# Small products of one pair of blocks and of the pair before in one stretch of TensorE's work instead of two

## The chip, the cores and the metric

The kernel runs on one core of a Trainium2 chip. The time is what the device needs for one launch, in microseconds; the lower the better. The median of three runs of the kernel before is 523.09 us (522.92 to 523.13).

## What is computed

A gated linear attention (4 batches, 8 heads, 768 steps, head size 48) whose output is the input of a feed-forward layer with a squared ReLU (3072 tokens, 384 wide, 2048 inside). q, k, v and alpha come as float32, the two weights as float64, which the kernel converts; the state of the attention is 48 x 48 for each batch and head.

```python
for t in range(S):
    state = alpha[:, :, t, :, None] * state + np.einsum('bhd,bhe->bhde', k[:, :, t], v[:, :, t])
    y[:, :, t] = np.einsum('bhd,bhde->bhe', q[:, :, t], state)
x = y.transpose(0, 2, 1, 3).reshape(B * S, H * D)
h = np.maximum(x @ w_in, 0.0)
return h * h @ w_out
```


## The kernel before

**Blocks and groups.** The 768 steps are cut into chunks of 128. A chunk of one batch is a block; there are 24, block n being chunk n // 4 of batch n % 4. Four blocks make a group of 512 tokens, and the six groups (g = 0 to 5 in the code, first to sixth in words) go one after the other through the feed-forward layer. The attention of the blocks of the next group is done in between, in pairs of blocks.

**The order is written out by hand.** Every instruction goes to its engine's queue in the order of the program text. The feed-forward layer of a group is a list of units with a cost (`layer_in`: 16 tiles of h, 1.05 + 0.53 each; then `layer_out` or `out_plain`: sums of the output, about 1.08 each). The attention of a pair is a list of events with a due time in the same units, made by `attention` from the table `PLAN` (`EARLY` for the first pairs). `weave` goes through the units and puts each event ahead of the first unit at whose start its time has come. A unit is near 1.3 us of TensorE in the first group, where products are plain float32, and in the later groups, which multiply three split parts. The numbers of the table `AT` are the starts of the pairs: in `'g': (2.2, 15.0)` those of two pairs in the third to fifth group.

**A pair in the attention.** `ln`, `sp`, `cs`, `eb`, `ei`, `mk`, `mq` turn alpha into running products and scale q and k by them; `turn` transposes q and k of both blocks (32 transposes of 64 x 64, L482), and ScalarE copies them out of PSUM. Then come the small products:

- `scores` (L365 to L375): 16 products a block, k against q, 48 x 64 by 48 x 64, into two PSUM banks called sckv;
- `state_sums` (L389 to L400): 16 products a block, k against v, into the other halves of the same two banks (8 in the last chunk of a batch, blocks 20 to 23);
- `masked`, `sums_copied`, `next_state`: VectorE takes the scores through a mask into `am`, adds the sums to the state (`us`), and makes the next state;
- y of a pair (`product` in `y_begin`, L349 to L357): 32 products with the states (`s`, `us`), 16 with the half of `am` that lies on the same rows (`inner` with h = e) and 16 with the other half (h = 1 - e), into two banks for the pair.

A product here is two weight loads and two matmuls in the records of TensorE. The second 16 of `inner` change the rows of TensorE that write a bank; an empty GpSimd instruction (L456) that waits for the last of the first 16, and that the first of the second 16 waits for, keeps them apart.

`ga(a, n)` issues scores, sums, mask and copy of block n, then y of pair a up to the first half of `inner`, then `next_state(n)`. `gb(a, n)` issues the second half of `inner` of pair a, and then all of the products of block n + 1. With n the first block of a pair and a = n - 2 the pair before, one pair makes two stretches of small products: `ga` at 10 units after the pair's start, `gb` at 12.5, with large products of the feed-forward layer between (2.35 times 9.5 and 10.5 units in the first group). After `gb` come the copies of y into x on ScalarE (`ev_part`, four parts of about three copies, L515). With `ga` and `gb` go loads on SP's queue: k of block n + 3, v of n + 2 and n + 3, k of n + 4, and they wait there until the tile that they overwrite has been read (three tiles of k, four of v).

PSUM has eight banks, all of one pool: a tile of h takes one, y of a pair two, a block's sckv two, the transposes four, and the output layer holds four through its whole length.

Of the kernel before, what the change touches and what calls it, by code (L numbers as in the profile page):

```python
# [15 lines left out]


GB = 4
AT = {'evs': 0.4, 'lead': 4, 'post': 3, 'w_first': (46.0, 49.5, 53.0), 'wstep': 1.6, 'w_in_at': 2, 'w_in_by': 3.4, 'room1': 22, 'room': 25, 's0': 4, 'ahead': 6, 'late': 2, 'xs': 0.2, 'g0': (-0.5, 19.5, 28.0), 'sc0': (2.35, 2.35, 2.35), 'g1': (2.5, 19.5, 35.0), 'g': (2.2, 15.0), 'g1x': 50, 'gx': 46, 'g0x': 55.5, 'k0': 2, 'h0': 18, 'k1': 4, 'h1': 4, 'h1by': 2, 'evs0': 0.8, 'tp': 'ADMD', 'tp1': 'ADAD', 'split': 8, 'o0': (40, 47), 'o1': (), 'o2': (23, 26, 29, 35, 42, 36), 'str1': 24, 'ga': 10, 'gb': 12.5}


RUN = {0: 128, 32: 32, 64: 64, 96: 32}
# [3 lines left out]
def kernel(  # L26
# [12 lines left out]
    nc = tc.nc  # L39
    B, H, S, D = q.shape  # L40
# [36 lines left out]
    NW = 8  # L77
# [384 lines left out]
    def gb(a, n):  # L462
# [7 lines left out]
        if n is not None:  # L470
            for f in (scores, state_sums, masked, sums_copied, next_state):
                f(n + 1)

    def turn(n):

        for m in (n, n + 1):
            ps = blk[m]["T"] = [bank(m, "T", (2, NP, 64)) for _ in range(2)]
            for i, x in enumerate("kq"):
                rows = tile_of(x, m).rearrange("a h d -> a (h d)")
                for p in range(NP):  # L480
                    for h in range(2):
                        nc.tensor.transpose(  # L482
                            out=ps[h][:, i, p, :], in_=rows[HALF[h], 128 * p : 128 * (p + 1)],
                            identity=ident[HALF[h], HALF[h]],
                        )
# [275 lines left out]
    def layer_out(g):  # L761
        posts = [(0, in_post, (n,)) for n in range(NJ + 2 - AT["post"], NJ)] if g else []
        plain = NW - AT["k0"] if g == 0 else NW - AT["k1"] if g == 1 else 0
        first = 2 * plain
        units = [(1, out_plain, (p, t, plain)) for p in range(plain) for t in range(GB)]
        if plain:
            for i, x in enumerate(posts):
                units.insert(1 + 2 * i, x)
            posts = []
        if plain == NW:  # L770
            for t in range(GB):
                units.append((0, lambda t: store(g, t, out_tile(t)), (t,)))
            return units
        ahead = AT["ahead"]
        split = [f for i in range(0 if plain else AHEAD, NJ - first) for f in splits_of_h(first, i)]
        if g == 0:
            split = [f for i in range(NJ - first) for f in [(0, split_h, (first + i, 0)), (0, diff_h, (first + i,))]]
        if plain:
            at = AT["h0" if g == 0 else "h1"]
            for i in range(min(AHEAD, len(split) // 2)):  # L780
                units[at:at] = split[0:2]
                del split[0:2]
                at += 2 + AT["h1by"]
        for _ in range(min(AT["s0"], len(split) // 2)):
            units += [split.pop(0), split.pop(0)]
        for n in range(first, NJ):
            units.append((1.08, out_x, (n, first)))
            if posts:
                units.append(posts.pop(0))
            while split and NJ - (len(split) + 1) // 2 <= n + ahead and (  # L790
                split[0][1] is diff_h or split[0][2][1] - AHEAD - MORE <= n - first
            ):
                units += [split.pop(0), split.pop(0)]
        ps = list(range(plain, NW))
        steps = [ps] if g == NG - 1 else [ps[i : i + 2] for i in range(0, len(ps), 2)]
        for pair in steps:
            units += [(0.27 * len(pair), out_y, (g, pair, t, pair[-1] == ps[-1])) for t in range(GB)]
        return units
# [87 lines left out]
        (3.0, "cs1 eb1 ei1"),  # L886
    ) + tuple(x for x in PLAN if x[0] > 3)

    def attention(pairs, scale):


        out = []
        for t, n0, after, *last in pairs:
            for at, fs in EARLY if n0 < SPLIT else PLAN:
                for f in fs.split():
                    w = t + (AT[f] if scale == 1 and f in ("ga", "gb") else at) * scale
                    if f in ("ga", "gb"):
                        given = n0 - 2 if after else None, None if last or n0 >= NBLK else n0
                        out.append((w, {"ga": ga, "gb": gb}[f], given))
                    if f == "gb" and after:  # L900
                        for p in range(NP):
                            out.append((w + AT["evs" if scale == 1 else "evs0"] * p, ev_part, (n0 - 2, p)))
                    if last:
                        continue
                    if f == "ga" and n0 + 3 < NBLK:
                        out.append((w, load, (n0 + 3, "k")))
                    elif f == "gb":
                        for m, x in ((n0 + 2, "v"), (n0 + 3, "v"), (n0 + 4, "k")):
                            if m < NBLK:
                                out.append((w, load, (m, x)))  # L910
                    elif f == "turn":
                        if n0 < NBLK:
                            out.append((w, turn, (n0,)))
                            for m in range(n0 + 2, min(n0 + 4, NBLK)):
                                out.append((w, load, (m, "q")))
                    elif f != "ga" and n0 < NBLK:
                        n = n0 + int(f[-1])
                        out.append((w, steps[f[:-1]], (n,)))
                        if f[:-1] == "cs" and n + 2 < NBLK:
                            out.append((w, load, (n + 2, "a")))  # L920
        return sorted(out, key=lambda x: x[0])

    def weave(units, events):
# [12 lines left out]
    def plain_out(g):  # L936
        n = NW - AT["late"]
        units = [(1, ffn_out, (g, t, i)) for i in range(n) for t in range(GB)]
        return units + [(1, ffn_out, (g, t, i)) for t in range(GB) for i in range(n, NW)]

    units = [(2, ffn_in, (0, j)) for j in range(2, NJ)]
    units += layer_out(0) if AT["k0"] else plain_out(0)
    events = [(3.4 * i, next_weights, (3 + i,)) for i in range(2 * NW - 3)]
    events += [(3.4 * i + 1.5, convert_second, (3 + i,)) for i in range(-1, 2 * NW - 3)]
    events += [(0, load, (GB + 1,)), (1.0, load, (GB + 2, "k"))]
    for p, at in enumerate(AT["w_first"]):
        events += prepare(at, "i", p)
    t0, t1, t2 = AT["g0"]
    for pair, scale in zip(((t0, GB, False), (t1, GB + 2, True), (t2, GB + 4, True) + (True,) * (len(AT["g1"]) == 3)), AT["sc0"]):
        events += attention([pair], scale)  # L950
    events += splits_of_x(AT["g0x"], 1)
    order = [*range(NW - AT["k0"], NW), *range(NW - AT["k1"], NW - AT["k0"])]
    order += range(NW - max(AT["k0"], AT["k1"]))
    for p, at in enumerate(AT["o0"]):
        events += prepare(at, "o", order[p])
    weave(units, sorted(events, key=lambda x: x[0]))
    hid.clear()
    acc.clear()

    def stream(g):  # L960
        if g == NG:
# [8 lines left out]
    def stream_out(n, xs="ld"):  # L970
        todo.extend((x, "o", p) for x in xs for p in range(NW - n, NW))
        pump()

    for g in range(1, NG):
        events = []
        if g + 1 < NG:
            n = GB * (g + 1) + 2
            *ts, t0, t1 = AT["g1" if g == 1 else "g"]
            pairs = [(t, n - 2, False) for t in ts] + [(t0, n, True), (t1, n + 2, True)]
            events += attention(pairs, 1)  # L980
            events += splits_of_x(AT["g1x" if g == 1 else "gx"], g + 1)
        if g == 1:
            m = len(AT["w_first"])
            for p in range(m, NW):
                events += prepare(AT["w_in_at"] + AT["w_in_by"] * (p - m), "i", p)
            for i, at in enumerate(AT["o1"] + AT["o2"]):
                events += prepare(at, "o", order[len(AT["o0"]) + i])
            n = min(AT["k0"], AT["k1"])
            todo.extend(("l", "o", p) for p in range(NW - n, NW))
            events.append((AT["str1"], stream_out, (AT["k1"], "d")))  # L990
        kinds[0] = AT["tp1" if g == 1 else "tp"]
        room[0] = AT["room1" if g == 1 else "room"]
        events.append((26, stream, (g + 1,)))
        events.sort(key=lambda x: x[0])
        weave(layer_in(g) + layer_out(g), events)
        if g == 1:
            w_out.clear()
            hid.clear()
            acc.clear()


# [28 lines left out]
```

## Time and profile before

The profiled execution and the runs:

| | us |
|---|---|
| median of three runs | 523.09 |
| span of the profiled execution, first to last instruction | 520.6 |
| TensorE busy in it | 510.8 |
| VectorE busy | 366.0 |
| ScalarE busy | 313.0 |
| mean granted TensorE clock | 1.000 of full speed |

The span leaves out what lies around the first and last instruction, so it stands 2.5 us below the median of the runs. The groups of instructions that the change moves, from the profile's fifth part:

| line | what | count | busy, us |
|---|---|---|---|
| L372 | matmuls of the scores | 768 | 16.5 |
| L395 | matmuls of the sums | 704 | 15.5 |
| L352 | matmuls of y, all forms | 1472 | 61.1 |
| L515 | copies of y on ScalarE | 132 | 47.2 |

Busy times of matmuls overlap and are not their share of the span; the starts are 6 to 15 ns apart within a stretch, against 174 ns for a 128 x 384 product of the output layer and 227 ns for a 128 x 512 product of the input layer. In the list of the chain that ended last, a line has the start in us, the duration in us, and engine, tile, line and count.

### The profile page before, as it was taken

The page shows a single profiled execution, that of the slowest core. Times are in us where ns is not written, and L with a number is a line of the kernel's source. Part 1 is how long each engine was busy: PE and PEld are TensorE (multiplying, and loading weights), DVE is VectorE, ACT ScalarE, POOL GpSimd, SP SyncE. Part 2 cuts the span into 40 slices and gives each one's busy share as a digit, 9 for nine tenths or more (in the row PEclk, how much of TensorE's full clock was granted, in tenths as well). Part 3 has the DMA queues.
Part 4 walks back from the last instruction along what each step waited for, and adds up shares of the span by engine and source line. Part 5 has one row for each costly group of instructions (what it writes and reads, how often), then busy time and mean ns, then how long its engine had stood idle before and what let it go on. Part 6 is the DMA issues. An engine that isn't in the chain of part 4 may idle for free.

```text
span 520.6 us, 12925 instructions
## 1 busy us (share of the span) xinstructions
PE 510.8 (98%) x5276; PEld 418.2 (80%) x5276; DVE 366.0 (70%) x631; ACT 313.0 (60%) x650; POOL 5.4 (1%) x29
## 2 busy tenths in 40 slices
PE   7989999999999999999999999999999999999997
PEld 4754455668887668988899988899988899988997
DVE  4798989979978787867597476587465476363861
ACT  4668785677888594575963275963275763164620
POOL 4000000000000000000000000000000000000000
PEclk9999999999999999999999999999999999999999
DMA  9999687244686787898884788964673534898201
GB/s 161 209 278 213 196 240 218 60 114 176 224 200 196 195 246 198 264 317 206 195 248 148 251 246 198 230 187 150 231 255 126 179 126 151 268 340 293 70 0 62
DMA packets 140995, 102.36 MB, mean 197 GB/s; under 512 B 111476, under 2 KB 114568, under 8 KB 140936
## 3 DMA queue, kind: packets, MB, share of 16 engines
q1 hardware_dynamic: 140936, 101.53, 68.3%
q8 instruction: 42, 0.69, 0.6%
q14 instruction: 17, 0.14, 0.1%
HBM read 84.18 MB, written 17.33 MB: 195 GB/s over the span
## 4 chain that ended last, share of the span: by engine, by line
PE 93%; DVE 2%; SPq 2%; DMA 1%; issue 1%; POOL 1%; ACT 0%; POOLq 0%; DVEq 0%
PE o L701 41%; PE h L622 32%; PE h L805 7%; PE y L352 4%; PE T L482 2%; PE sckv L372 2%; PE sckv L395 2%; PE cs L265 1%; DMA qk_lent<-in_q_dram 1%; SPq L303 1%; SPq L109 1%; PE cs L268 1%; PE cs L269 1%; DVE x L515 0%; DVE w_in L182 0%
## 5 line engine op out<-in xcount | busy, mean ns | idle before, releaser
L622 PE MATMUL h<-xa,wb 128*128 128x512 f32 x240 | 68.2, 392 | 0.0
L622 PE MATMUL h<-xl,wl 128*128 128x512 f32 x240 | 67.9, 391 | 0.0
L622 PE MATMUL h<-xd,wd 128*128 128x512 f32 x240 | 67.3, 396 | 0.0
L515 ACT COPY x<-y 32x256 f32<-32x256 f32 (+2 forms) x132 | 47.2, 366 | 25.4 <-PE y L352 20.1
L547 DVE TENSOR_TENSOR hid<-h,hid 128x512 f32<-128x512 f32 x40 | 27.6, 689 | 45.5 <-PE h L622 45.4
L701 PE MATMUL o<-wb,ha 128*128 128x384 f32 x160 | 54.6, 342 | 0.0
L701 PE MATMUL o<-w_out,hid 128*128 128x384 f32 x160 | 54.0, 491 | 0.0
L701 PE MATMUL o<-wd,hd 128*128 128x384 f32 x304 | 53.8, 334 | 0.0
L701 PE MATMUL o<-wl,hl 128*128 128x384 f32 x160 | 53.5, 335 | 0.0
L639 ACT ACTIVATE h<-h 128x512 f32<-128x512 f32 x40 | 23.3, 582 | 49.7 <-PE h L622 49.7
L622 PEld LDWEIGHTS h<-xl,wl 128*128 128x128 f32 x240 | 45.1, 188 | 10.0 <-DVE xl L547 0.4
L701 PEld LDWEIGHTS o<-wd,hd 128*128 128x128 f32 x304 | 52.7, 188 | 0.3 <-DVE osb L737 0.3
L622 PEld LDWEIGHTS h<-xa,wb 128*128 128x128 f32 x240 | 44.6, 188 | 9.3 <-ACT xa L596 0.2
L622 PEld LDWEIGHTS h<-xd,wd 128*128 128x128 f32 x240 | 44.2, 188 | 9.2
L701 PE MATMUL o<-wb,hx 128*128 128x384 f32 x144 | 48.7, 338 | 0.0
L701 PE MATMUL o<-wl,hx 128*128 128x384 f32 x144 | 48.1, 334 | 0.0
L701 PEld LDWEIGHTS o<-w_out,hid 128*128 128x128 f32 x160 | 29.8, 190 | 19.3
L637 ACT ACTIVATE hid<-h 128x512 f32<-128x512 f32 x40 | 24.0, 600 | 34.6 <-PE h L622 34.5
L805 PE MATMUL h<-x,w_in 128*128 128x512 f32 (+1 forms) x108 | 43.6, 552 | 1.2 <-ACT x L515 1.2
L596 ACT ACTIVATE ha<-hid 128x512 fp32r<-128x512 f32 x40 | 25.6, 639 | 25.5 <-DVE hx L547 16.1
L805 PEld LDWEIGHTS h<-x,w_in 128*128 128x128 f32 x108 | 19.9, 190 | 21.1 <-issue 17.2
L547 DVE TENSOR_TENSOR hl<-hid,ha 128x512 fp32r<-128x512 f32 x40 | 27.5, 688 | 10.1 <-ACT ha L596 10.1
(114 smaller groups left out, 879.7 us busy)
## 6 DMA issues: line engine op xcount, KB each, us to landing
wd<-do SPq DMA_DIRECT2D x36, 384.0 KB, 3.7
wl<-lo SPq DMA_DIRECT2D x34, 384.0 KB, 4.0
wl<-li SPq DMA_DIRECT2D x32, 384.0 KB, 3.5
wd<-di SPq DMA_DIRECT2D x32, 384.0 KB, 3.9
raw<-in_moe_w_in_dram SPq DMA_DIRECT2D x8, 768.0 KB, 5.6
raw<-in_moe_w_out_dram SPq DMA_DIRECT2D x8, 768.0 KB, 5.6
v_in<-in_v_dram SPq DMA_DIRECT2D x24, 192.0 KB, 4.7
out_dram<-osb SPq DMA_DIRECT2D x24, 192.0 KB, 1.9
```

What stands on the lines that cost most here:

```text
L352: ins = nc.tensor.matmul(out=ys[e][64 * half : 64 * half + D + G * e, m % 2, p // 2, t], lhsT=lhsT, rhs=rhs, start=(half, e) not in seen, ...
L372: nc.tensor.matmul(out=ps[e][HALF[h], 0, p, :], lhsT=ks[rows, p, HALF[h]], rhs=qs[rows, p, HALF[h]], start=True, stop=True, skip_group_che ...
L395: nc.tensor.matmul(out=ps[h][64 * e : 64 * (e + 1), 1, p, G:64], lhsT=tile_of("k", n)[HALF[h], 2 * p + e, :], rhs=tiles["v"][n % NV][HALF[ ...
L482: nc.tensor.transpose(out=ps[h][:, i, p, :], in_=rows[HALF[h], 128 * p : 128 * (p + 1)], identity=ident[HALF[h], HALF[h]],)
L515: copy(out=x[kk][to : to + m, t : t + 2], in_=blk[n]["y"][e][r : r + m, :, p // 2],)
L547: nc.vector.tensor_tensor(out=o, in0=x, in1=z, op=op)
L596: nc.scalar.activation(out=a, in_=x, func=AF.Copy, scale=NEAR)
L622: nc.tensor.matmul(out=acc["h", j], lhsT=here[w, "i", p][:, kk, jj * 128 : (jj + 1) * 128], rhs=x_parts[x][:, kk], start=start and kk == 0 ...
L637: nc.scalar.activation(out=hid[j], in_=x, func=AF.Copy, scale=E)
L639: nc.scalar.activation(out=x, in_=x, func=AF.Copy, scale=1.0 + E)
L701: nc.tensor.matmul(out=acc[t][:, 0:DM], lhsT=lhs[:, t * C : (t + 1) * C], rhs=rhs, start=start, stop=stop, skip_group_check=True,)
L805: nc.tensor.matmul(out=ps, lhsT=w[:, kk, c0 : c0 + 128], rhs=xT[g][kk][:, cols], start=(kk == 0), stop=(kk == KM - 1),)
```

## The change

A new function `joined(a, n)` issues in one go what `ga` and `gb` did in two: the banks of y are taken first, then scores and sums of block n, y of pair a up to the first half of `inner`, `next_state(n)`, scores and sums of block n + 1, the second half of `inner`, and `next_state(n + 1)`. Where there is no n it calls `ga` and `gb` one after the other.

`attention` now takes one pair, with a time `whole_at`: where it is given, `joined` stands at that time, and the loads and copies of y that went with `ga` and `gb` go with it; where it is not, `ga` and `gb` stay. The table says for which:

- first group: blocks 4 and 5 at unit 27 (`ga` was at 21.8, `gb` at 24.2); blocks 6 and 7 and the y of 6 and 7 stay as they are;
- second group: blocks 8 and 9 at 12.5 (12.5 and 15.0); blocks 10 and 11 with the y of 8 and 9 at 24.8, and the preparation of 10 and 11 starts at 15.0, not at 19.5 (29.5 and 32.0); blocks 12 and 13 stay as they are;
- third to fifth group: the first pair at 12.2 (12.2 and 14.7), the second at 24.8 (25.0 and 27.5); in the fifth group the second has no new block, only y.

All groups are now woven in one list, with the units' start of the group added to the times, and what was done between two groups (emptying tables, setting the kinds of tiles) are units that cost nothing.

```diff
-AT = {... 'g0': (-0.5, 19.5, 28.0), ... 'g1': (2.5, 19.5, 35.0), 'g': (2.2, 15.0), ...}
+AT = {... 'g0': ((-0.5, 4, False, True, 27), (19.5, 6, True, True), (28.0, 8, True, False)),
+      ... 'g1': ((2.5, 8, False, 12.5), (15.0, 10, True, 24.8), (35.0, 12, True)),
+      'g': ((2.2, 6, True, 12.2), (15.0, 8, True, 24.8)), ...}
...
+    def joined(a, n):
+
+        if n is None:
+            ga(a, None)
+            gb(a, None)
+            return
+        product = y_begin(a) if a is not None else None
+
+        def sums(m):
+            for f in (scores, state_sums, masked, sums_copied):
+                f(m)
+
+        sums(n)
+        if a is not None:
+            for h in range(1 if a < B else 0, 2):
+                for m, p, e in heads(a):
+                    rows = slice(64 * e, 64 * e + D)
+                    s = blk[m]["u" if h else "s"]
+                    product(m, p, e, s[rows, p, G * (1 - e) : 64], blk[m]["qs"][rows, p, HALF[h]], HALF[h])
+            for m, p, e in heads(a):
+                end = inner(product, m, p, e, e)
+            passed = nc.gpsimd.nop(nofuse=True)
+            dep(passed, end)
+        next_state(n)
+        sums(n + 1)
+        if a is not None:
+            for i, (m, p, e) in enumerate(heads(a)):
+                begin = inner(product, m, p, e, 1 - e)
+                if i == 0:
+                    dep(begin, passed)
+        next_state(n + 1)
...
-    def attention(pairs, scale):
+    def attention(t, n0, after, scale=1, begun=True, whole_at=None, turn_at=None):
...
+                if f in ("ga", "gb") and whole_at is not None:
+                    w = whole_at
...
+                if f == "ga":
+                    out.append((w, ga if whole_at is None else joined, given))
+                elif f == "gb":
+                    if whole_at is None:
+                        out.append((w, gb, given))
+                    if after:
                         for p in range(NP):
-                            out.append((w + AT["evs" if scale == 1 else "evs0"] * p, ev_part, (n0 - 2, p)))
+                            out.append((w + AT["evs" if scale == 1 else "evs0"] * p, ev_part, (old, p)))
...
+                if f == "ga":
+                    loads(w, (n0 + 3, "k"))
+                elif f == "gb":
+                    loads(w, (n0 + 2, "v"), (n0 + 3, "v"), (n0 + 4, "k"))
...
-        weave(layer_in(g) + layer_out(g), events)
...
+    weave(units, sorted(events, key=lambda x: x[0]))
```

More of the change, by code (lines that the diff above doesn't have):

```diff
@@ L18 @@
 GB = 4
-AT = {'evs': 0.4, 'lead': 4, 'post': 3, 'w_first': (46.0, 49.5, 53.0), 'wstep': 1.6, 'w_in_at': 2, 'w_in_by': 3.4, 'room1': 22, 'room': 25, 's0': 4, 'ahead': 6, 'late': 2, 'xs': 0.2, 'g0': (-0.5, 19.5, 28.0), 'sc0': (2.35, 2.35, 2.35), 'g1': (2.5, 19.5, 35.0), 'g': (2.2, 15.0), 'g1x': 50, 'gx': 46, 'g0x': 55.5, 'k0': 2, 'h0': 18, 'k1': 4, 'h1': 4, 'h1by': 2, 'evs0': 0.8, 'tp': 'ADMD', 'tp1': 'ADAD', 'split': 8, 'o0': (40, 47), 'o1': (), 'o2': (23, 26, 29, 35, 42, 36), 'str1': 24, 'ga': 10, 'gb': 12.5}
+AT = {'evs': 0.4, 'lead': 4, 'post': 3, 'w_first': (46.0, 49.5, 53.0), 'wstep': 1.6, 'w_in_at': 2, 'w_in_by': 3.4, 'room1': 22, 'room': 25, 's0': 4, 'ahead': 6, 'late': 2, 'xs': 0.2, 'g0': ((-0.5, 4, False, True, 27), (19.5, 6, True, True), (28.0, 8, True, False)), 'sc0': (2.35, 2.35, 2.35), 'g1': ((2.5, 8, False, 12.5), (15.0, 10, True, 24.8), (35.0, 12, True)), 'g': ((2.2, 6, True, 12.2), (15.0, 8, True, 24.8)), 'g1x': 50, 'gx': 46, 'g0x': 55.5, 'k0': 2, 'h0': 18, 'k1': 4, 'h1': 4, 'h1by': 2, 'evs0': 0.8, 'tp': 'ADMD', 'tp1': 'ADAD', 'split': 8, 'o0': (40, 47), 'o1': (), 'o2': (23, 26, 29, 35, 42, 36), 'str1': 24, 'ga': 10, 'gb': 12.5}
 RUN = {0: 128, 32: 32, 64: 64, 96: 32}
@@ L887 @@
     ) + tuple(x for x in PLAN if x[0] > 3)
-    def attention(pairs, scale):
+    def attention(t, n0, after, scale=1, begun=True, whole_at=None, turn_at=None):
         out = []
[L893 to L900, printed above, removed]
-                        for p in range(NP):
-                            out.append((w + AT["evs" if scale == 1 else "evs0"] * p, ev_part, (n0 - 2, p)))
[L903 to L920, printed above, removed]
@@ new lines, in attention, with loads @@
+        old = n0 - 2 if after else None
+        given = old, n0 if begun and n0 < NBLK else None
+        def loads(at, *which):
+            out.extend((at, load, (m, x)) for m, x in which if m < NBLK)
+        for at, fs in EARLY if n0 < SPLIT else PLAN:
+            for f in fs.split():
+                w = t + (AT[f] if scale == 1 and f in ("ga", "gb") else at) * scale
+                if f in ("ga", "gb") and whole_at is not None:
+                    w = whole_at
+                if f in ("turn", "kc0", "kc1", "qc0", "qc1", "br0", "br1") and turn_at is not None:
+                    w = turn_at + (at - 6.5) * scale
+                if f == "ga":
[4 more added lines that the diff above has]
+                    if after:
+                        for p in range(NP):
+                            out.append((w + AT["evs" if scale == 1 else "evs0"] * p, ev_part, (old, p)))
+                if not begun:
+                    continue
+                if f == "ga":
+                    loads(w, (n0 + 3, "k"))
+                elif f == "gb":
+                    loads(w, (n0 + 2, "v"), (n0 + 3, "v"), (n0 + 4, "k"))
+                elif n0 >= NBLK:
+                    continue
+                elif f == "turn":
+                    out.append((w, turn, (n0,)))
+                    loads(w, (n0 + 2, "q"), (n0 + 3, "q"))
+                else:
+                    n = n0 + int(f[-1])
+                    out.append((w, steps[f[:-1]], (n,)))
+                    if f[:-1] == "cs":
+                        loads(w, (n + 2, "a"))
@@ L939, in plain_out, with ended, begun @@
         return units + [(1, ffn_out, (g, t, i)) for t in range(GB) for i in range(n, NW)]
[L941 to L958, printed above, removed]
+    def ended(g):
+        hid.clear()
+        acc.clear()
+        if g == 1:
+            w_out.clear()
+    def begun(g):
+        kinds[0] = AT["tp1" if g == 1 else "tp"]
+        room[0] = AT["room1" if g == 1 else "room"]
     def stream(g):
@@ L972, in stream_out @@
         pump()
-    for g in range(1, NG):
-        events = []
-        if g + 1 < NG:
[L977 to L981, printed above, removed]
+    units = [(2, ffn_in, (0, j)) for j in range(2, NJ)]
+    units += layer_out(0) if AT["k0"] else plain_out(0)
+    units.append((0, ended, (0,)))
+    base = [0]
+    events = [(3.4 * i, next_weights, (3 + i,)) for i in range(2 * NW - 3)]
+    events += [(3.4 * i + 1.5, convert_second, (3 + i,)) for i in range(-1, 2 * NW - 3)]
+    events += [(0, load, (GB + 1,)), (1.0, load, (GB + 2, "k"))]
+    for p, at in enumerate(AT["w_first"]):
+        events += prepare(at, "i", p)
+    order = [*range(NW - AT["k0"], NW), *range(NW - AT["k1"], NW - AT["k0"])]
+    order += range(NW - max(AT["k0"], AT["k1"]))
+    for p, at in enumerate(AT["o0"]):
+        events += prepare(at, "o", order[p])
+    events += splits_of_x(AT["g0x"], 1)
+    for (t, n0, after, run, *other), scale in zip(AT["g0"], AT["sc0"]):
+        events += attention(t, n0, after, scale, run, *other)
+    for g in range(1, NG):
+        base.append(sum(u[0] for u in units))
+        at0 = base[g]
+        units.append((0, begun, (g,)))
+        units += layer_in(g) + layer_out(g)
+        units.append((0, ended, (g,)))
+        if g + 1 < NG:
+            for t, n0, after, *other in AT["g1"] if g == 1 else AT["g"]:
+                n0 = n0 if g == 1 else n0 + GB * g
+                other = [None if x is None else at0 + x for x in other]
+                events += attention(at0 + t, n0, after, 1, True, *other)
+            events += [(at0 + t, f, x) for t, f, x in splits_of_x(AT["g1x" if g == 1 else "gx"], g + 1)]
         if g == 1:
@@ L984 @@
             for p in range(m, NW):
-                events += prepare(AT["w_in_at"] + AT["w_in_by"] * (p - m), "i", p)
+                events += prepare(at0 + AT["w_in_at"] + AT["w_in_by"] * (p - m), "i", p)
             for i, at in enumerate(AT["o1"] + AT["o2"]):
-                events += prepare(at, "o", order[len(AT["o0"]) + i])
+                events += prepare(at0 + at, "o", order[len(AT["o0"]) + i])
             n = min(AT["k0"], AT["k1"])
[L989 to L994, printed above, removed]
-        weave(layer_in(g) + layer_out(g), events)
[L996 to L999, printed above, removed]
+            events.append((at0, lambda: todo.extend(("l", "o", p) for p in range(NW - n, NW)), ()))
+            events.append((at0 + AT["str1"], stream_out, (AT["k1"], "d")))
+        events.append((at0 + 26, stream, (g + 1,)))
+    weave(units, sorted(events, key=lambda x: x[0]))
 _INS = ['q', 'k', 'v', 'alpha', 'moe_w_in', 'moe_w_out']
```

## The prediction

> **What bounds the kernel now.** I read the page first, then the chain that ended last, then the timeline of TensorE in single stretches, and last the packets of the instruction queue.
>
> ```profile
> span 520.6 us, 12925 instructions
> ...
> PE 510.8 (98%) x5276; PEld 418.2 (80%) x5276; DVE 366.0 (70%) x631; ACT 313.0 (60%) x650; POOL 5.4 (1%) x29
> ...
> q8 instruction: 42, 0.69, 0.6%
> ...
> PE 93%; DVE 2%; SPq 2%; DMA 1%; issue 1%; POOL 1%; ACT 0%; POOLq 0%; DVEq 0%
> ```
>
> TensorE is busy throughout and is 93% of the chain: a microsecond taken from its order of work, or put into it, is one of the whole. The q8 line is how TensorE's program arrives: 42 packets of 0.69 MB, 16,384 bytes each; 10,702 recorded TensorE instructions over 42 is 255 a packet. I take blocks of 256.
>
> The chain at one stretch of the second group and two of the third, with a long run of plain work for comparison:
>
> ```profile
> 200.56 0.62 PE sckv L372 x32
> 201.19 0.45 PE sckv L395 x32
> 201.64 1.45 PE y L352 x86
> 203.09 0.96 issue
> 204.05 0.33 PE y L352 x3
> 204.38 3.00 PE o L701 x16
> ...
> 235.99 0.62 PE sckv L372 x32
> 236.62 0.45 PE sckv L395 x32
> 237.07 1.41 PE y L352 x92
> 238.49 2.95 PE h L622 x12
> 241.43 0.62 PE y L352 x31
> 242.06 0.46 PE sckv L372 x32
> 242.52 0.46 PE sckv L395 x30
> 242.98 4.32 PE h L622 x18
> ...
> 451.09 32.68 PE h L622 x144
> ```
>
> Two things are to be seen: what a break between small and large products costs, and a stop of 0.96 us that no semaphore ends.
>
> **What is saved.** The change drops one break per joined pair. The first 32 matmuls of a stretch take 0.62, the next 32 about 0.46: 0.16 for coming in. The 12 large ones between the two halves take 2.95 us against 12 x 32.68/144 = 2.72: 0.23 for getting going and draining. Together 0.39; by starts alone I read 0.36; I take 0.38. Nine stretches are joined: blocks 4 and 5 (first group), 8 and 9, and 10 and 11 (second), 14 and 16 (third), 18 and 20 (fourth), 22 and the y of 22 alone (fifth). In the last nothing stands between the two halves of y, and the wait for GpSimd's empty instruction (L456), hidden before by large products, is laid open: at 30.18 us, where the two halves already adjoin, that gap is 0.34. So eight breaks count: -3.0 us. In the others the 64 matmuls of the second block (0.92 us) hide the 0.34. Nothing is queued behind that instruction on GpSimd.
>
> **What is paid: instructions.** A product is two weight loads and two matmuls. A full joined stretch holds 128 products, 512 instructions, two whole blocks, in about 3.9 us (from block 20 on, where kv has one half, 448); before, the halves held 320 and 192, with 2.9 to 4.4 us of large products between.
>
> ```profile
> 204.05 0.19 PEld L352 LDWEIGHTS y<-am,v_in 64*48 64x48 f32 x3 [1.10 <-issue]
> ```
>
> The stop at 202.87 (1.18 us between starts) falls behind the 4,544th TensorE instruction, which is 18 x 256 - 64. With borders at 256k - 64, the fetches that fall into long runs of large products begin mostly 18 to 36 instructions ahead of their border, from 53 us to 513 us without drift: the count holds. The stretch at 200.49 is the only one of the old kernel that meets two borders (at its instructions 59 and 315) with small products alone between them. At the first border the fetch began 0.78 us after it was passed, took 0.96, and TensorE ran on 1.40 us after its end; small products reach the next border in 1.96. So the stop is 0.78 + 0.96 + 1.40 - 1.96 = 1.18. The stretch at 174.23 also has two (36 and 292), but its first was fetched before the stretch began, and nothing stops.
>
> Up to the start of each joined stretch the same TensorE instructions have run as before the old first half (some waits apart), so the borders are known, and for five of them the fetch itself is in the trace of before:
>
> - group 2, blocks 10 and 11: moved to stand before the output layer, five units of eight instructions earlier than at 174.23; border at 76, second at 332: with the 0.6 to 1.1 seen in most dense stretches, 1.2 us.
> - group 3, first: border at 213; 1.09 + 0.93 + 1.40 - 1.95 = 1.5. Second: border at 247; its own fetch began only 3.18 us after the border, with four weight transfers under way, which gives 3.8; from the smallest row (0.61, 0.88) 0.9. I take 2.2, nearer the other stretches, since the border is nine instructions from wrapping out of the stretch and a transfer there will start later.
> - group 4: borders at 142 and 176; 1.4 and 1.5.
> - group 5, first: border at 134; 0.61 + 0.88 + 1.40 - 1.95 = 0.9, I take 0.8 for its fewer kv products.
>
> The three short stretches (256 instructions) cross one border each: 0. Sum +8.6; ends 5.0 and 10.5. The stop at 200.49 belongs to a pair that stays in two stretches; I leave it.
>
> [...]
>
> **What is paid: banks and queues.** A stretch now holds six PSUM banks (two y, four sckv) beside three of h at unit 12.2: nine of eight. The last sckv takes a bank of the first block's, free when its sums are copied: in the trace 237.79 + 0.35 = 238.14 (VectorE L406), and TensorE would want it at 235.92 + 2.39 = 238.31. Cost 0; without that cover, 0.2 to 0.7 per stretch if VectorE is behind by one 0.69 us instruction.
>
> At unit 24.8 the copies of y (L515, 0.37 each, three to a part) come from 27.5 to 24.8 and two parts now stand on ScalarE ahead of the ReLU of h14 and of four splits of h, all waiting for the end of y. From the end of the stretch: 0.25 + 2.2 for copies, 0.6 ReLU (L656), 0.6 split, 0.69 VectorE rest: the fourth split is ready after 4.3 us; TensorE has three output units of 8 x 33.32/192 = 1.39 us (o L701 at 483.77 in the chain), with the start 4.3. So it arrives just in time, and with VectorE's 1.38 us per split plus one 0.69 post the eighth comes 0.4 late. Between 0 and 0.6 in groups 3, 4 and 5: +0.6, ends 0 and 1.8.
>
> SP: the two v loads and one k load move with the second half; v overwrites the v that the stretch reads (four tiles), so SP waits there, at unit 24.8 instead of 27.5, and one wd load behind it (issued at 260.84 before) comes some 2 us later; it is read in the last quarter of the layer, over 20 us on. Cost 0. In the first group the k load of block 7 goes from unit 21.8 to 27, three units (4 us) ahead of its multiply against a landing of 4.7 us; VectorE has over 5 us of weight conversion queued ahead of it there. Cost 0; uncovered, 1.
>
> Blocks 10 and 11 are prepared 4.5 units earlier, inside the loaded input layer of group 2. The old preparation of blocks 8 and 9 in that layer shows idle of 0.26 (transposes, 141.74) and about 0.3 (cumulative sums, 135): 0 to 0.6, I take 0.3. The single weave over all groups changes no order but of events that tie: 0.
>
> **Sum.** -3.0 + 8.6 + 0.6 + 0.3 = +6.5 us on a span of 520.6: 527.1. The median of the runs, 523.09, lies 2.5 above the span; so 529.6. Ends: 5.0 - 3.0 = +2.0, 525.1; 10.5 + 1.8 + 0.6 - 3.0 = +9.9, 533.0.
>
> **Rivals.** (1) Fetching hides behind the stretch, the stop at 203 us was something else or needs a rarer coincidence. For: only one stop in the trace; it is put down to nothing. Against: its place to the instruction and the fetch just before it. Then 523.1 - 3.0 + 0.6 + 0.3 = 521.0, down to 520.1. Faster. It decides if the second border costs under 0.3 us per stretch. (2) Fetches stop TensorE, but for less: half the borders have shifted by added or dropped waits, or the request goes out earlier in a longer stretch. Then +8.6 is 2 to 4, and the time 522.2 to 525.1. Against: at 134 to 213 the borders lie 40 and more instructions from where the stop vanishes (about 40 and 256). (3) The output layers of groups 3 to 5 starve behind the ScalarE queue, each 1.5 us and more, on top of the stops: 533.5. For: ScalarE is strictly in order, and stands idle 4.60 us at 265.88 only because its work was done early; against: the sum above meets the need within 0.4.
>
> **How the numbers follow.** Forecast 0.74, range 525.1 to 533.0; rival 1 0.14; rival 2 0.08; rival 3 0.04. The range that leaves out no more than 2 in 10 reaches from rival 2's lower end, 522.0, to 533.0. What differs by under 0.2% (1.05 us) can't be told from no change here. Faster: rival 1, 0.14. Same: the lower part of rival 2 and the upper edge of rival 1, 0.04. Slower: 0.82.
>
> **What would show it.** Right: six new pieces of "issue" of 0.8 to 3 us inside y or sckv of full stretches, none in the three short ones, each behind an instruction 256k - 64 and 1.4 us after a packet of q8 ends; one run of large products fewer per pair; h L622 and o L701 as before. Wrong: full stretches of 3.9 us without a gap, or gaps ended by a semaphore (VectorE: banks; GpSimd: L456; ScalarE: splits). The forecast is wrong most simply if TensorE holds more than two blocks.

## The result, and the profile after

The changed kernel takes 539.73 us (median of four runs, 537.10 to 541.26) against 523.00 for the kernel before on the same chip (522.41 to 523.13): a ratio of 1.0315, 95% interval 1.0285 to 1.0345. It is slower by 16.7 us. The profiled execution took 537.1, its span is 535.3: 14.7 more than before. The page, with the parts that were shown of before:

```profile
span 535.3 us, 12918 instructions
...
PE 513.1 (96%) x5276; PEld 418.6 (78%) x5276; DVE 366.1 (68%) x631; ACT 314.5 (59%) x650; POOL 5.4 (1%) x29
...
q8 instruction: 42, 0.69, 0.5%
...
PE 76%; DVE 8%; ACT 6%; issue 4%; DMA 2%; SPq 2%; DVEq 0%; POOLq 0%
```

No engine has more instructions than before, and TensorE is busy for 513.1 us against 510.8, yet its share of the chain fell from 93% to 76%. The rest is of two kinds: "issue" (4%, before 1%), and stretches in which the chain runs through VectorE and ScalarE (8% and 6%, before 2% and 0%). Through most of the latter TensorE still works, and only the wait at the end of each costs time. Both are to be seen in the chain through the third group:

```profile
239.42 1.35 PE y L352 x88
...
242.02 1.08 issue
243.11 0.58 PE y L352 x18
...
248.87 0.94 ACT a_in L244 x2
...
251.46 0.57 DVE lo L257
...
252.07 0.44 PE cs L269
252.52 5.48 PE h L654 x24
258.00 1.16 PE T L514 x32
259.15 4.34 PE h L654 x18
...
267.35 2.77 issue
270.12 0.33 PE y L352 x3
```

**The stops.** All six full joined stretches stop once, and each stop lies behind an instruction 256k - 64 of TensorE, the second border of the stretch. Between starts they last 1.35 us (at 171.20, second group), 1.30 (241.80) and 2.98 (267.13, third), 2.10 (325.98) and 2.44 (352.47, fourth) and 0.98 (411.03, fifth): 11.15 together. The old stop, now at 205.44, is 1.08. The three short joined stretches have none.

**The waits behind the stretches.** TensorE's own timeline after the first of these stops (start, duration, operation and, in brackets, idle time and what ended it):

```profile
250.57 0.34 PE L268 MATMUL cs<-hi,causal_r 128*128 128x384 f32 x1
250.74 0.34 PE L269 MATMUL cs<-lo,causal_r 128*128 128x384 f32 x1
251.48 0.44 PE L268 MATMUL cs<-hi,causal_r 128*128 128x384 f32 x1 [0.40 <-DVE hi L256]
252.07 0.44 PE L269 MATMUL cs<-lo,causal_r 128*128 128x384 f32 x1
```

Four cumulative sums of the next pair follow at steps of 0.17 us where nothing is late (as at 251.54 in the run with one joined pair below); here two steps are 0.74 and 0.59, a loss of 1.0. At 336.18 the same comes again (0.79 and 0.59, 1.04). What they wait for stands on ScalarE. First before, then after:

```profile
240.79 0.60 ACT L637 ACTIVATE hid<-h 128x512 f32<-128x512 f32 x1 [4.18 <-PE h L622]
241.29 0.93 ACT L244 ACTIVATE a_in<-a_in 128x384 f32<-128x384 f32 x2
242.24 1.13 ACT L515 COPY x<-y 32x256 f32<-32x256 f32 x3
```

```profile
243.71 3.33 ACT L547 COPY x<-y 32x256 f32<-32x256 f32 x9 [4.74 <-PE y L352]
247.06 0.60 ACT L669 ACTIVATE hid<-h 128x512 f32<-128x512 f32 x1
247.69 1.15 ACT L547 COPY x<-y 64x256 f32<-64x256 f32 x3
248.87 0.94 ACT L244 ACTIVATE a_in<-a_in 128x384 f32<-128x384 f32 x2
```

Before, the logarithm of alpha (`a_in`, L244) stood ahead of the copies of y, and ScalarE did it while TensorE ran the second stretch (from 241.43 in the chain of before). Now ScalarE has nothing to do for the whole joined stretch (idle 4.74 us), and then everything at once: twelve copies (4.5 us), and the logarithm behind them. From the end of y at 243.69 to the end of `lo` at 252.03 that is 8.3 us; TensorE has 30 large products in between, 6.9 us. The whole-trace list of waits says the same: ScalarE's copies waited 43.5 us for y, before 20.1.

In the output layers of the third to fifth group a product waits for a split of h, 0.43 us above the step of 0.17 each time (the other two at 365.08 and 441.45):

```profile
280.24 0.34 PE L733 MATMUL o<-wb,ha 128*128 128x384 f32 x1
280.85 0.44 PE L733 MATMUL o<-wl,hl 128*128 128x384 f32 x1 [0.27 <-DVE hl L579]
```

**By group.** From the starts of the first product of each layer: second group +2.3 us, third +5.5, fourth +5.7, fifth +1.2, sixth 0, first -0.5, and +0.5 ahead of the first layer: 14.7. The last is scatter: the change alters nothing there, and the first layer begins between 27.2 and 28.4 us over all the profiles here.

### The profile page after: what moved, and what is told of

The parts are those of the page before. It is cut to its first block, busy times and chain, and to the rows that moved or that the text cites. A ratio compares the mean times of both kernels' runs of the same rounds, so it can differ in the third digit from the quotient of the medians.

```text
span 535.3 us, 12918 instructions
## 1 busy us (share of the span) xinstructions
PE 513.1 (96%) x5276; PEld 418.6 (78%) x5276; DVE 366.1 (68%) x631; ACT 314.5 (59%) x650; POOL 5.4 (1%) x29
## 4 chain that ended last, share of the span: by engine, by line
PE 76%; DVE 8%; ACT 6%; issue 4%; DMA 2%; SPq 2%; DVEq 0%; POOLq 0%
PE o L733 33%; PE h L654 25%; PE h L837 7%; PE y L352 4%; ACT x L547 3%; PE T L514 2%; PE sckv L372 2%; PE sckv L395 1%; SPq L303 1%; DMA qk_lent<-in_q_dram 1%; DVE hx L579 1%; PE cs L265 1%; SPq L109 1%; DVE hd L632 1%; DVE hid L579 1%
## 5 line engine op out<-in xcount | busy, mean ns | idle before, releaser
L547 ACT COPY x<-y 32x256 f32<-32x256 f32 (+2 forms) x132 | 47.0, 366 | 48.8 <-PE y L352 43.5
L579 DVE TENSOR_TENSOR hl<-hid,ha 128x512 fp32r<-128x512 f32 x40 | 27.5, 687 | 7.4 <-ACT ha L628 7.4
```

The lines of the kernel that those rows point to most:

```text
L547: copy(out=x[kk][to : to + m, t : t + 2], in_=blk[n]["y"][e][r : r + m, :, p // 2],)
L579: nc.vector.tensor_tensor(out=o, in0=x, in1=z, op=op)
```

## The experiments

The theory: a stretch of small products that holds two instruction borders runs to the second before the next 256 instructions have come, and stops. It was tried by moving borders, in the changed kernel and in the kernel before; then the joins were cut down, and last the transfers beside a fetch were moved.

**Empty instructions ahead of the stretches.**

```diff
+        for _ in range(n):
+            nc.tensor.nop(nofuse=True)
...
+    for g, at, k in [(1, 0, 62), (1, 48, 138), (2, 14, 32), (2, 27, 150), (3, 14, 32), (3, 27, 213)]:
+        events.append((base[g] + at, pad, (k,)))
```

> The changed kernel with 627 empty TensorE instructions, at most two behind each large product, so that the 256-instruction borders fall near instruction 18 of each of the six full joined stretches (62, 138, 32, 150, 32 and 213 ahead of them). Fetch theory: the six stops of 1.0 to 3.0 us (11.1 in the trace) and the old one (1.1) all but vanish, the span goes from 535.3 to 523 to 525 and the time to 525 to 528. Rival, a wait for banks or for GpSimd: the stops stay where they are by product, at the same places of the stretch, and the time stays at 537 to 541 or grows by what the empty instructions cost.

Measured 538.19 (536.02 to 540.45), ratio 1.0296 [1.0258, 1.0335]. It tells nothing of borders: the profiled program has 12,918 instructions in 42 packets, as the changed kernel has. The empty instructions were not in it, and the stops lie behind the same instructions. It is a repeat of the changed kernel, and as such of use: the stop at 267.12 lasted 3.81 us here and 2.98 there, the two of the fourth group 1.51 and 1.38 here and 2.10 and 2.44 there, and the six together 10.4 and 11.15.

The same edit in the kernel before, 155 empty instructions:

```diff
+        events += [(at, pad, (k,)) for h, at, k in [(1, 48, 155)] if h == g]
```

> The kernel before with 155 empty TensorE instructions near the end of its second group, so that in its first stretch of the third group (320 instructions) the first border moves from 213 to 58 and a second one to 314. Fetch theory: a new stop of 1.0 to 1.8 us in y some 2.3 us after the start of that stretch, the one in the second group stays, time 524 to 525. Rival: no stop there, 522.5 to 523.5.

522.67 in a single run, 12,925 instructions as before, no new stop: inconclusive for the same reason.

**Copies of y later.** They come 2.5 units after a joined stretch, as far from its second half as in the kernel before.

```diff
-                            out.append((w + AT["evs" if scale == 1 else "evs0"] * p, ev_part, (old, p)))
+                            late = 0 if whole_at is None else 2.5
+                            out.append((w + late + AT["evs" if scale == 1 else "evs0"] * p, ev_part, (old, p)))
```

> The changed kernel with the copies of y 2.5 units later, where they stood before (14.7 and 27.5), stretches unchanged. Theory that ScalarE's order costs what the stops do not explain: the waits for the cumulative sums (1.3 at 251, 1.4 at 336) and the output layers' 0.6 at 280, 365 and 441 go, 3 to 5 us less than the changed kernel, 534 to 537; the stops stay. Rival, that the rest is only a consequence of the stops: no change, 538 to 541.

536.57 (536.27 to 536.99), ratio 1.0266 [1.0250, 1.0281]: 3.2 us under the changed kernel's first measurement, 1.6 under its repeat on this chip, whose interval overlaps this one. What the order on ScalarE costs in time is therefore not settled by this run, but its profile shows the waits. Those for splits in the output layers are gone, and with the logarithm ahead of the copies again so are the waits for the sums near 251 and 336 us. But in their place a product of h starts 0.98 us after the one ahead of it, at 251.01 (0.75 above its step), and again at 338.45. What ends its wait is a copy of y, the seventh of nine that now stand in a row on ScalarE:

```profile
252.00 0.95 PE L654 MATMUL h<-xa,wb 128*128 128x512 f32 x3 [0.65 <-ACT x L547]
```

The bunch on ScalarE is waited for at either place. The stop at 266.84 grew to 4.88 us in this execution, in the chain:

```profile
267.05 4.67 issue
271.72 0.33 PE y L352 x3
```

With the empty instructions as well, which again are not in the program, it is a repeat:

> Both edits. If the two causes add: 12 plus 3 to 5 less than the changed kernel, 521 to 525, at the time of the kernel before or under it. If the second is a consequence of the first: as with the borders moved alone, 525 to 528.

536.82 (533.61 to 538.18), ratio 1.0249 [1.0209, 1.0290]; the longest stop 3.94. The six stops sum to 11.4 and 12.0 in these two profiles.

**Borders moved by aligning addresses.** Instead of empty instructions, the program's addresses are aligned ahead of each full joined stretch, so that its first border lies at the stretch's instruction 18 or 19.

```diff
+    for g, at, k in [(1, 21.6, 200), (2, 9.0, 200), (2, 21.6, 200), (3, 9.0, 200), (3, 21.6, 200), (4, 9.0, 200)]:
+        events.append((base[g] + at, lambda k: nc.tensor.addr_align(256, offset=k, max_nops=0), (k,)))
```

> The changed kernel with six directives that align TensorE's program, each about 38 instructions ahead of a full joined stretch: slots up to the next place are filled and branched over, so that the first border lies at instruction 18 or 19 of the stretch, where large products still stand before it. (The empty instructions of the earlier runs never came into the loaded program.) Fetch theory: the six stops (11.1 us in the trace) fall to under 0.5 us each, the one at 205 goes too since its border moves to 3; span 523 to 526, time 524 to 529. Rival, banks or GpSimd: the stops stay at the same products, 536 to 541.

530.91 (528.16 to 533.42), ratio 1.0163 [1.0130, 1.0196]: 7.7 us above the kernel before, where it had been 16.7, without a change to any product, though not down to the 529 that was the upper end of the expectation. The program now takes 44 packets instead of 42. The second border now lies at instruction 275, and the stops there are 0.45, 0.16, 0.69, 1.45 and 1.13, with none in the sixth stretch; but the stretch ends only 20 instructions ahead of a third border, and TensorE stops there, in the middle of large products, 1.28, 1.15 and 1.28 us in three cases. The chain at the first stretch of the third group:

```profile
239.13 0.45 PE y L352 x31
239.58 1.81 PE h L654 x7
241.39 0.89 issue
242.28 0.85 PE h L654 x3
```

That a run of large products stops at the border too, once the fetch is late, is the strongest sign that the small products are not the cause as such, only the pace. Neither place of the borders that was tried keeps a stretch of 512 instructions free of stops.

> The same with the copies of y 2.5 units later as well. If ScalarE's order has a price of its own: 1 to 4 us less than with the directives alone, 520 to 525. If not: the same as those within 1.

Both edits together: 530.06 (528.32 to 530.34), ratio 1.0124 [1.0104, 1.0144]. The waits of 0.97 for a copy of y are back (249.49 and 331.37), the waits in the output layer gone. The 520 to 525 that was expected if ScalarE's order has a price of its own didn't come, and the 0.85 us to the run before are within the noise.

**The same in the kernel before, both ways.** One address is aligned there, so that the stretch of blocks 12 and 13 has its borders at 20 and 276 instead of 59 and 315:

```diff
+        events += [(at, lambda k: nc.tensor.addr_align(256, offset=k, max_nops=0), (k,)) for h, at, k in [(1, 42.6, 203)] if h == g]
```

> The kernel before with one directive, 33 instructions ahead of its only stretch that stops (200.49 in its trace), border from 59 to 20. Fetch theory: that stop of 1.2 us goes and nothing else changes, 521.3 to 522.2. Rival, the stop has another cause: 522.5 to 523.5 and a gap of 1 us there.

521.53 (521.20 to 521.73) against 523.24, ratio 0.9967 [0.9955, 0.9979]: 1.7 us faster, 1.1 to 2.4, where the stop in the profile was 1.18. It is gone; the chain of waits now runs through that stretch without a pause:

```profile
201.06 0.62 PE sckv L372 x32
201.68 0.45 PE sckv L395 x32
202.13 1.44 PE y L352 x90
203.57 2.98 PE o L701 x16
```

And the opposite: a stretch of the third group that never stopped gets its borders at 58 and 314.

```diff
+        events += [(at, lambda k: nc.tensor.addr_align(256, offset=k, max_nops=0), (k,)) for h, at, k in [(2, 9.0, 160)] if h == g]
```

> The kernel before with one directive ahead of the first stretch of the third group, border from 213 to 58, the second at 314 of 320. Fetch theory: a stop of 1.0 to 1.8 us at the border in that stretch, which has none in the kernel before, and 523.7 to 525. Rival: no gap there, 522.5 to 523.5.

526.16 in a single run (before 523.24). The stop is there, in a stretch of the old form, in the place the theory names (the chain of waits):

```profile
237.68 1.41 PE y L352 x89
239.09 0.96 issue
240.05 0.33 PE y L352 x4
240.38 2.76 PE h L622 x11
```

All later borders shifted with it, so two others were hit as well (0.98 at 265.55, in large products, and 0.85 at 343.21); the three together are 3.0, and the time rose by 2.9. With that the cause of the stops is shown from both sides: the stop comes and goes with the border. The jump over the skipped places that each alignment adds (one recorded branch) isn't the cause, since the same edit took a stop away in the run before.

**Joins that cost no fetch.** Only the two joined stretches of 256 instructions with new blocks are kept, blocks 4 and 5 and blocks 8 and 9.

```diff
-AT = {... 'g1': ((2.5, 8, False, 12.5), (15.0, 10, True, 24.8), (35.0, 12, True)), 'g': ((2.2, 6, True, 12.2), (15.0, 8, True, 24.8)), ...}
+AT = {... 'g1': ((2.5, 8, False, 12.5), (19.5, 10, True), (35.0, 12, True)), 'g': ((2.2, 6, True), (15.0, 8, True)), ...}
```

> The changed kernel's table with the four-field entries only where a joined stretch has 256 instructions and one instruction border: blocks 4 and 5 (first group) and 8 and 9 (second group). All other pairs stand in two stretches as before. Theory (stops come only where two borders lie within small products; a break is worth 0.38 us): no new stop, two breaks less, -0.8 us: 522.3 to 522.8 at a before of 523.1, the old stop near 203 us still there at 1.0 to 1.3. Rival A (joining costs by itself, through the loads, the copies or the single weave): 523.5 to 525. Rival B (the break is worth more than 0.38, so that the gain is over 2 us): under 521.5.

521.92 (11 runs, 521.40 to 523.41) against 522.57 (17 runs), ratio 0.9988 [0.9979, 0.9997]: 0.65 us faster, 0.2 to 1.1. Two breaks at 0.38 are 0.76. The chain through the stretch of blocks 8 and 9, in one piece:

```profile
146.38 0.62 PE sckv L372 x32
147.00 0.45 PE sckv L395 x32
147.45 0.48 PE sckv L372 x32
147.93 0.45 PE sckv L395 x32
148.39 3.63 PE h L654 x15
```

With the aligned address for blocks 12 and 13 on top:

> The same, and the border in the stretch of blocks 12 and 13 moved from instruction 59 to 20, so that the second lies behind the stretch, as in the run in which the kernel before gained 1.7 us by it. Theory: both gains add, -0.8 - 1.7 = -2.5 us: 520.4 to 521.2, no stop in any stretch. Rival A (joining costs by itself): 521.5 to 523. Rival B (break worth more): under 520.

520.65 (520.24 to 521.12), ratio 0.9961 [0.9949, 0.9972]: 1.9 us faster than before (1.5 to 2.7), where 2.5 was expected. It is the lowest median here, though its interval overlaps that of the old kernel with the aligned address alone. No small product stands more than 0.55 us apart from the next after the first group.

**One full join alone.** Blocks 14 and 15 with y of 12 and 13, all other pairs in two stretches (the table's other times for joining are taken out, which isn't shown).

```diff
+                if n0 == 14:
+                    other = [12.2]
```

> The changed kernel with a single pair joined: blocks 14 and 15 with y of 12 and 13, in the third group (512 instructions, borders at some 213 and 469). Theory: one break less (-0.4), one stop of 1.2 to 1.6 us at the second border, and behind it 0.5 to 1.0 us of waits for the cumulative sums of the next pair, whose inputs stand on ScalarE behind the delayed copies of y: +1.3 to +2.2, 524.4 to 525.3 at a before of 523.1. Rival A (the waits have nothing to do with the stop but with stretches joined in the groups ahead): +0.8 to +1.2. Rival B (joining one pair gains, and only several in a row lose): 522.7 or less.

525.50 (524.87 to 528.20), ratio 1.0062 [1.0043, 1.0081], +2.9 us, 2.2 to 4.2: at the median more than any of the three had said. The stop is 2.45 us between starts (2.24 of it "issue" in the chain) and not 1.2 to 1.6, its fetch began 1.99 us after its border, and after the stop the clock falls. Busy times by stretch (TensorE, its weight loads, VectorE, ScalarE, GpSimd), then granted clock, DMA share and GB/s:

```profile
240.10:242.40 2.30, 0.06 (x4) 0.02 (x3) 2.23 (x6) 0.00 (x0) 0.00 (x0) 1.00 0.74 211
242.40:245.90 3.50, 3.50 (x28) 2.81 (x29) 0.00 (x0) 2.49 (x8) 0.00 (x0) 0.51 0.59 117
245.90:251.50 5.60, 5.60 (x26) 4.63 (x25) 2.88 (x6) 5.00 (x11) 0.00 (x0) 1.00 0.80 248
```

The clock record has a piece of 3.41 us at half speed from 242.49, of which half, an estimated 1.7, is lost where TensorE is busy throughout. In the three runs whose clock stayed at 1.000 the time is 524.87 to 525.26. The wait for the sums can't be seen here, as the slowed products cover it: 30 of them took 8.29 us instead of 6.9, and the last `hi` was ready 7.85 us after y. So this run does not tell whether those waits need the joins ahead.

**What makes a fetch late.** In the changed kernel's profile the fetch began 0.45 to 0.65 us after its border in three of the six stretches and in the old one that stops, and 2.56, 1.54 and 1.97 in the other three. Between border and fetch the DMA share was 0.10 to 0.60 in the former and 0.82 to 0.94 in the latter; the 0.00 to 0.34 and 0.73 to 1.03 of the expectation below come from other stretches of time. So the weights that SP's queue issued just ahead of these three stretches were held back until behind the loads of v.

```diff
-        while todo and todo[0] in stored and len(here) + len(made) + 2 * NW - len(cut) < room[0]:
+        while todo and not held[0] and todo[0] in stored and len(here) + len(made) + 2 * NW - len(cut) < room[0]:
...
+    for g, a, b in ((2, 20.0, 24.81), (3, 7.5, 12.21), (3, 20.0, 24.81)):
+        events += [(base[g] + a, hold, (True,)), (base[g] + b, hold, (False,))]
```

> The changed kernel, and the transfers of weights that SP's queue issued just ahead of three joined stretches (third group's second, fourth group's first and second) are held back until behind the loads of v that follow the stretch. In the changed kernel the fetch began 2.56, 1.54 and 1.97 us after its border in these three, where the DMA share was 0.73 to 1.03, against 0.45 to 0.65 in the others, where it was 0.00 to 0.34. Theory (a fetch of instructions starts late when weight transfers are under way): it begins 0.4 to 1.0 after the border in all three, the stops fall from 2.98, 2.10 and 2.44 to 1.2 to 1.6, no half-clock stretch, and the time falls by 3 to 5 us against the changed kernel's 539.7: 534.5 to 537. Rival A (the delay belongs to the place in the program and not to the transfers): stops as in the changed kernel, 538 to 540.5. Rival B (held weights come late and are waited for): new waits of TensorE for DMA in the input or output layer, over 540.5.

534.21 (533.33 to 534.93), ratio 1.0222 [1.0208, 1.0236]: 5.5 us less than the changed kernel, a little more than expected. The fetches began 1.17, 1.08 and 1.10 after their borders, and the three stops are 1.66, 1.55 and 1.40 instead of 2.98, 2.10 and 2.44. The same columns as above, from the border at 265.24 to its fetch in the changed kernel, and then from the same border, now at 264.31, with the weights held:

```profile
265.24:267.80 2.56, 2.11 (x144) 1.97 (x136) 1.97 (x7) 0.00 (x0) 0.00 (x0) 1.00 0.94 330
```

```profile
264.31:265.48 1.17, 1.17 (x97) 1.17 (x91) 1.03 (x4) 0.00 (x0) 0.00 (x0) 1.00 0.60 122
```

At this border 330 GB/s stand against 122, and the fetch comes in half the time. Here the transfers hold it up: in the four profiles without the hold it began 2.56 to 4.39 us after its border. For the two stretches of the fourth group the run shows nothing of the kind. Without any hold, the repeat of the changed kernel has 0.90 and 0.87 there, the two runs with later copies 0.80 to 1.06, and the stops were 1.28 to 1.89. Nor does a busy DMA always make a fetch late. First the fourth group's first border in the repeat, then the same border with the weights held:

```profile
325.84:326.74 0.90, 0.90 (x78) 0.90 (x74) 0.74 (x3) 0.00 (x0) 0.00 (x0) 1.00 1.07 397
```

```profile
321.83:322.91 1.08, 1.08 (x90) 1.08 (x86) 0.92 (x3) 0.00 (x0) 0.00 (x0) 1.00 0.00 0
```

So what else sets the delay, and why it isn't 0.45 here, stays open. Not all of the 5.5 us is due to the hold, either: 3.8 lie between the two profiled executions, both at a clock of 1.000, and 1.4 of these had come before the third group began, ahead of any held weights.

## Why the prediction was right or wrong

The direction was right, and so was the mechanism of the stops. The size was not: 529.6 was said, with 533.0 as the end of the range, and it is 539.7. The step that failed is the price of the stops, +8.6 with 10.5 as its end, where 11.15 was measured; and two costs stood in no step, the logarithm behind the copies on ScalarE in the input layers (2.0) and the fallen clock (1.9 in the median). By the steps of the prediction:

- **Breaks, -3.0.** Held where it could be seen alone: two breaks gave 0.65 us, 0.76 by the prediction's price.
- **Stops, +8.6, ends 5.0 and 10.5: mis-sized.** All six came where they were said, and none in the short stretches, but they sum to 11.15 (10.4 to 12.0 over the four profiles with these stretches). Three were close: 1.2 said and 1.35, 1.5 and 1.30, 0.8 and 0.98. The other three were 2.2 and 2.98, 1.4 and 2.10, 1.5 and 2.44: 2.4 too little. For these I took the delay of a fetch from quiet stretches, or leaned towards them, although the one row with transfers under way (3.18 us after its border) was in front of me. Holding the weights back made the one of 2.98 shorter by 1.3. That the other two were so long belongs to this execution: in three others with the same stretches they lay between 1.28 and 1.89.
- **Banks, 0.** In the chain through the six stretches nothing but the stops interrupts the products.
- **Output layers, +0.6, ends 0 and 1.8.** 1.3 (three times 0.43), in the range.
- **Preparation of blocks 10 and 11, +0.3.** It cost about 1.2 at 155 us, where VectorE makes hi and lo behind weight pieces, and some 0.4 at 190. The first is not there in every execution: with the weights of later groups held, the same products follow without it. The 0.3 that I read in the cumulative sums of before at 135 us isn't there: from 134.72 their steps are 0.17 to 0.20.
- **What was not in the sum.** I followed the earlier copies of y into the output layer only. In the input layers of the third and fourth group they also overtook the logarithm of the next pair on ScalarE, which costs 1.0 each. The chain of copies and logarithm is counted from the end of y, as TensorE's own work is, so the wait shouldn't need the stop; but no run shows it without one. With the borders moved, the stop that then falls behind y covers it. With the 0.5 ahead of the first layer and a remainder of about 1.2, which may be small waits or breaks worth less than 0.38, the waits come to 6.6, where the sum had 0.9.
- **The span to the median, +2.5.** The profiled execution kept its clock at 1.000 and lies only 1.8 above its span; the other three had 0.991 to 0.994 and took 1.8 to 4.2 us longer. The granted clock fell after some long stops, as the profiles of the repeats show (0.50 for 3.41 us behind the stop of 3.81 at 267.12), and the old kernel's profile has no such piece. So the median is 2.6 above the profiled execution.

On the span: 527.1 was said and 535.3 came, 8.2 more: 2.6 of stops and 5.7 of waits, less 0.1 at the old stop. The median adds 1.9. The stops alone would have left the time at 532.2, inside the range.

Of the rivals, the first (fetches hidden) is ruled out by the run in which an old stretch was made to stop, and the second (smaller stops) by the sizes. The third (output layers starve, 533.5) had the right engine, ScalarE, and the wrong place: the price fell due mostly in the input layer. A fetch took from its border 0.6 + 1.1 + 1.5 = 3.2 us in a quiet stretch (second group) and 2.6 + 1.0 + 1.3 = 4.9 beside weight transfers (third). In both places the small products ran from one border to the next in 1.9 us, and the rest was paid: 1.35 and 2.98. In the old kernel's stretch of blocks 12 and 13, with its borders at 20 and 276 instead of 59 and 315, nothing was paid, where it had been 1.18. No run shows by itself how many blocks TensorE holds; in the seven stops of the changed kernel's profile the packet that ended the stop began 0.45 to 2.56 us after the border ahead.

## What to carry to other kernels

Before merging dense runs of short instructions, count them: find where the fetch borders lie, and see how long the engine needs from one border to the next (here 1.9 us in small products) against the time that a fetch takes (here 3.2 to 4.9), from its slowest row and with the transfers that will be under way. Where the count doesn't fit, keep large products between, or try to move the border by aligning an address, which gave 1.7 us in the old kernel for one line and cost 2.9, in a single run, in another place. And a stretch that is made longer on one engine can leave those it feeds without work, as ScalarE here, idle for 4.74 us: read what stood between the two halves not only as cost but as their work.

## What the runs showed of the hardware

- From the end of the packet to the next instruction 1.28 to 1.63 us pass in the seven stops of the changed kernel's profile, and 1.40 in the one of before; the packet itself takes 0.88 to 1.8. What varies most is its start: 0.4 to 4.4 us after the border in the full joined stretches that were left where they were.
- A stop of TensorE inside a run may cost twice. In five of the profiled executions' stops, of 1.78 to 4.88 us, a stretch of 3.41 us at half clock began within 0.9 us of the end of the stop, by which an estimated 1.7 us, half of it, are lost each time, if TensorE is busy throughout; it did not after stops of 2.98 and 2.44 in the changed kernel's own profile. Why like stops end differently is not shown.
- Empty instructions on TensorE's queue did not reach the loaded program: with 627 of them it had 12,918 instructions in 42 packets, as without. Alignments of addresses moved the borders: with six of them it had 44 packets, and the second border lay at instruction 275 of the full joined stretches.
